# Opening of an attention and feed-forward kernel: order of the first tile's products, count of warm transposes, place of GpSimd's first subtractions, table of the loads' landing

## The chip, the cores and the metric

The kernel runs on one core of a Trainium2 chip. A core has five engines with queues of their own: TensorE (matrix products and transposes into PSUM), VectorE, ScalarE, GpSimd and SyncE (SP), which issues most transfers. The metric is the time of one execution in microseconds (us) of device time, the median over several runs. In the profile's rows TensorE is PE (its weight load is PEld), VectorE DVE, ScalarE ACT, GpSimd POOL.

## What is computed

The reference normalizes x and feeds it to two branches, a dilated local attention and a feed-forward network with SiLU:

```python
def _A_ref(x, wqkv, wo):                     # H = 32 heads of 20, W = 8 keys, dil = 2
    q, k, v = split(x @ wqkv)
    logits = jnp.einsum("bhsd,bhswd->bhsw", q, kg) * scale      # kg: keys at s, s-2, ..., s-14
    attn = _softmax(jnp.where(mask, logits, -1e9), axis=-1)
    o = jnp.einsum("bhsw,bhswd->bhsd", attn, vg)
    return merge(o) @ wo

def _B_ref(x, w1, w2):
    return jnp.einsum("bsf,fd->bsd", _silu(jnp.einsum("bsd,df->bsf", x, w1)), w2)

xn = _layernorm(x, axis=-1)
s = _A_ref(xn, A_wqkv, A_wo)
g = _silu(_B_ref(xn, B_w1, B_w2))
return x + s * g
```

x is 2048 x 640, wqkv 640 x 1920, w1 640 x 1536, everything float32.

## The kernel before

**Groups and tiles.** The 2048 tokens are worked in four groups of 512, each of four tiles (T = 4) of 128 tokens. In a group come four quarters of the q, k, v product (eight heads each, 480 columns), with the attention of each quarter on VectorE; then the feed-forward network, and the output product of the group before. TensorE's order is the order in which the program adds its work.

**Three products for one.** A float32 operand is split into a high part, rounded for TensorE, and a low part, the difference. Each product is done as high x high, low x high and high x low. For activations the parts are `th` and `tl`: ScalarE copies a transposed tile from PSUM into th (L674), VectorE subtracts (L678). For weights ScalarE copies the loaded tile into the high half of a ring tile `w` (L445), and VectorE or GpSimd subtracts into its low half (L451). The ring has seven tiles; in the built program they are called w_75 to w_81, and the first five chunks of the first quarter lie in w_75 to w_79. Chunks 0 and 1 are subtracted by GpSimd, chunks 2, 3, 4 by VectorE (`ON_DVE`).

**The opening** (`first_quarter`). TensorE first turns the identity 20 times (`WARM`, L644). Meanwhile x of the first tile lands in two halves, one issued by SP and one by ScalarE. `begin(t)` puts a tile's layer norm on VectorE: two statistics (L656), their aggregate (L657), a square root on ScalarE (L495), a reciprocal (L497), and the normalization itself (L661) in two parts, of three and two chunks of 128 columns. `turn(t)` transposes the five chunks on TensorE (L670) into two PSUM tiles, and queues the copies into th and tl. `products(t, steps)` adds products (L691); a step (k, c) is pass k (0: th with the high weight, 1: tl with the high weight, 2: th with the low weight) of chunk c. For tile 0 the order is th and tl of each chunk in turn; between tile 1's transposes and its first product stand `NOW` products of pass 2 of tile 0.

**The planner.** `Weave` collects every operation with its engine, a modelled duration, the keys that it reads and writes and a priority, and sorts each engine's queue by a modelled time line; `emit` then writes the instructions in that order. The keys serve the planner alone: the semaphores in the built program are set by the framework below it, from the memory that instructions really share. Each engine's queue is in order. A transfer's end is modelled from its bytes (`RATE`), a constant (`LAND`), and a correction for early ones (`EARLY`). Operations marked `lock` are modelled as excluding each other between VectorE and GpSimd.

**Transfers.** SP issues, in the opening, x of tile 0 (half), weight chunk 0, x of tile 1, chunks 2 to 4, x of tile 2, two chunks of the next quarter (`xr`, for w_80 and w_81), x of tile 3, four more (`gate`), then stores of split weights (`half_q`) and further loads. ScalarE issues the other half of x and weight chunk 1. There are eight lanes: a transfer waits on SP until the one eight places before it has landed.

Of the kernel before, what the change touches and what calls it, by code (L numbers as in the profile page):

```python
# [8 lines left out]
F32 = mybir.dt.float32  # L9
F32R = mybir.dt.float32r  # L10
AF = mybir.ActivationFunctionType
OP = mybir.AluOpType
# [10 lines left out]
T = 4  # L23
# [7 lines left out]
NS = 3  # L31
SINGLE = 6
RAW_AHEAD = 10
WARM, WARM2 = 20, 3
HOLD = 3.4
LO = 10
HALVES = 1
BY_ACT = (1,)
QAT = 48
MORE = 32  # L40
# [1 line left out]
X_AT = 3, 6, 8  # L42
TILE_AT = 1, 1.5, 5, 6
LOW_AT = 3
NOW = 1
ON_DVE = (2, 3, 4)


# [16 lines left out]
class Weave:  # L65
# [8 lines left out]
    LANES = 8  # L74
    RATE = 310e3
    LAND = 1.9
    EARLY = 10.0, -0.4
    TABLE = 1.28
    PATIENCE = 1.0

# [28 lines left out]
    def order(self):  # L109
        engines = ("PE", "POOL", "DVE", "ACT", "SP")  # L110
        free = dict.fromkeys(engines, 0.0)
        can = {e: [] for e in engines}
        tensor = [o for o in self.ops if o.eng == "PE"]
        at = 0
        lock = dma = 0.0
        lanes = {e: [0.0] * self.LANES for e in ("SP", "POOL", "ACT")}
        table = held = None
        for o in self.ops:
            if o.left == 0:
                can[o.eng].append(o)  # L120
        done = []
        while len(done) < len(self.ops):
            best = None
            for e in engines:
                if e == "PE":
                    c = [tensor[at]] if at < len(tensor) and tensor[at].left == 0 else []
                else:
                    c = can[e]
                if not c:
                    continue  # L130
                f = free[e]
                est = [max(f, o.ready, lock if o.lock else 0.0, lanes[e][0] if o.nbytes else 0.0) for o in c]
                m = min(est)
                if best is None or m < best[0] or (m == best[0] == lock and held == best[1].eng):
                    pick = min((o for o, t in zip(c, est) if t <= m + 1e-9), key=lambda o: (o.prio, o.seq))
                    if pick.prio >= 140:
                        soon = [(t, o.prio, o.seq, o) for o, t in zip(c, est)
                                if o.prio < 100 and t <= m + min(self.PATIENCE, pick.dur / 2)]
                        if soon:
                            m, _, _, pick = min(soon, key=lambda v: v[:3])  # L140
                            if best is not None and m >= best[0]:
                                continue
                    best = m, pick
            t, o = best
            e = o.eng
            o.start = t
            dur = o.dur
            if e == "ACT" and o.table is not None and o.table != table:
                table = o.table
                dur += self.TABLE  # L150
            free[e] = t + dur
            if o.nbytes:
                dma = max(dma, t + dur) + o.nbytes / self.RATE
                o.end = dma + self.LAND + (self.EARLY[1] if lanes[e][-1] and t < self.EARLY[0] else 0.0)
                lanes[e] = lanes[e][1:] + [o.end]
            else:
                o.end = t + dur
                if o.lock:
                    lock, held = o.end, e
            if e == "PE":  # L160
                at += 1
            else:
                can[e].remove(o)
            done.append(o)
            for u in o.users:
                u.left -= 1
                u.ready = max(u.ready, o.end + (self.HOP if u.eng != e or o.nbytes else 0.0))
                if u.left == 0:
                    can[u.eng].append(u)
        self.span = max(o.end for o in done)  # L170
        return sorted(done, key=lambda o: (o.start, o.seq))
# [7 lines left out]
def local_attention_silu_ffn(ctx: ExitStack, tc: tile.TileContext, x, wqkv, wo, w1, w2, out):  # L179
# [80 lines left out]
    def dve(n, fn, reads, writes, prio, lock=False):  # L260
        add("DVE", dv(n), fn, reads, writes, prio, lock)
# [4 lines left out]
    def pe(dur, fn, reads, writes):  # L266
        add("PE", dur, fn, reads, writes)
        clock[0] += dur
# [152 lines left out]
    def w_load():  # L421
        i = loaded[0]
        if i >= len(units):
            return
        loaded[0] += 1
        u, s = units[i], i % RING
        n = width(i)
        r = WR[s]
        at = start(i)
        both = r.rearrange("p (s d) -> p s d", s=2)[:, :, at:at + n]  # L430
        whi, wlo = both[:, 0], both[:, 1]
        kh, kl = ("wh", s), ("wl", s)
        due = clock[0]
        if what[i] == "load":
            src = halves[u]
            add("POOL", 1.0, lambda: nc.gpsimd.dma_start(both, src), [("half", u), ("half", u, "more")], [kh, kl], due + 10,  # L436
                nbytes=2 * n * P * 4)
            raws_due(i, sum(j < i for j in fresh) - 1)
            return
        k = fresh.index(i)  # L440
        if not k:
            raw_load(0)
            rawn[0] = 1
        raw, kr = raws.pop(i)
        act(n, lambda: nc.scalar.activation(whi, raw, AF.Copy), kr + [("sd", 0)] * (k < 2), [kh], 1000 + due)  # L445
        pool_does = k < LO and k not in ON_DVE
        eng, cost, by = ("POOL", po(n), nc.gpsimd) if pool_does else ("DVE", dv(n), nc.vector)
        parts = HALVES if pool_does and k < DC else 1
        for j in range(parts):
            cs = slice(j * n // parts, (j + 1) * n // parts)  # L450
            add(eng, po(n // parts) if pool_does else cost, lambda cs=cs: by.tensor_tensor(  # L451
                out=wlo[:, cs], in0=raw[:, cs], in1=whi[:, cs].bitcast(F32), op=OP.subtract), [kh] + kr,
                [kl if j == parts - 1 else kl + (j,)], due if pool_does else LOW_AT if k < LO else 50, lock=True)
        if what[i] == "store":
            def keep(to, a, b, key):
                dma(lambda: nc.sync.dma_start(to, both[:, :, a:b].bitcast(F32)), [kh, kl], [key], 2 * (b - a) * P * 4,
                    due + 25)
            wide = width(len(units) - 1 - units[::-1].index(u))
            kept = dram.tile([P, 2, wide], F32, name="half_" + "_".join(map(str, u)))
            halves[u] = kept  # L460
            past = n - wide if u[0] == "q" and u[1] == NQ - 1 else 0
            keep(kept[:, :, :n - past], past, n, ("half", u))
            for k in range(past // MORE):
                v = ("q", k, u[2])
                keep(halves[v][:, :, 3 * CQ:], k * MORE, (k + 1) * MORE, ("half", v, "more"))
        raws_due(i, k)
# [26 lines left out]
    def ln_rstd(a, b, at=1):  # L493
        n = range(a, b)
        act(b - a, lambda: nc.scalar.activation(SD[:, 0, a:b], MV[:, a:b, 1], AF.Sqrt, bias=epst, scale=1.0),  # L495
            [("mv", t) for t in n], [("sd", t) for t in n], 0, "sqrt")
        dve(10, lambda: nc.vector.reciprocal(out=SD[:, 1, a:b], in_=SD[:, 0, a:b]),  # L497
            [("sd", t) for t in n], [("rs", t) for t in n], at)
# [139 lines left out]
    def first_quarter(i):  # L638
# [3 lines left out]
        def warm(n, where):  # L642
            for k in range(n):
                nc.tensor.transpose(where[:, tsl(k % T)], ident, ident)  # L644
        pe(4.5, lambda: warm(WARM, ROT[0]), ["consts"], [("rot", 0)])

        PARTS = (0, 3), (3, DC)

        def begin(t):

            at = TILE_AT[t]
            st, ks = ST[t % 2], ("st", t % 2)
            for k in range(2):
                cs = slice(k * 320, (k + 1) * 320)
                kx = ("xin", t) if t or k else ("xin", t, "a")
                dve(320, lambda k=k, cs=cs: nc.vector.bn_stats(out=st[:, k, :], in_=XIN[:, t, cs]), [kx], [ks + (k,)], at)  # L656
            dve(60, lambda: nc.vector.bn_aggr(out=MV[:, t, :], in_=st), [ks + (0,), ks + (1,)], [("mv", t)], at)  # L657
            ln_rstd(t, t + 1, at)
            for j, (a, b) in enumerate(PARTS):
                cs = slice(a * P, b * P)  # L660
                dve((b - a) * 64, lambda cs=cs: nc.vector.tensor_scalar(  # L661
                    out=XIN[:, t, cs], in0=XIN[:, t, cs], scalar1=MV[:, t, 0:1], scalar2=SD[:, 1, t:t + 1],
                    op0=OP.subtract, op1=OP.mult), [("rs", t), ("mv", t), ("xin", t)], [("xn", t, j)], at, lock=True)
# [50 lines left out]
            ps[t] = b, kp  # L714
        turn(0)
        pe(0.11 * WARM2, lambda: warm(WARM2, ACC[5]), [], [("acc", 5)])
        products(0, [(k, c) for c in range(DC) for k in (0, 1)])
        turn(1)
        products(0, [(2, c) for c in range(NOW)])
        products(1, passes(0, 1))  # L720
# [292 lines left out]
```

## Time and profile before

| | |
|---|---|
| time, median of 3 runs | 637.09 us (636.86 to 637.24) |
| time of the profiled execution | 638.26 us |
| its span (first to last instruction) | 636.5 us |
| TensorE busy | 629.1 us, 99% of the span, 3495 products |
| VectorE busy | 545.8 us, 86%, 548 instructions |
| ScalarE busy | 224.0 us, 35% |
| GpSimd busy | 114.6 us, 18% |

A row of the time line gives the start, the duration (of all merged instructions), engine, line, operation, written tile <- read tiles, shape, and xN for N merged instructions; brackets give the idle time before it and what ended it. A row of waits reads "engine line waited for: us in total, times, longest us". A row of windows gives the stretch, its length, then the busy time and the number of instructions of PE, PEld, DVE, ACT and POOL, then the granted TensorE clock (1.00 is full), the share and the rate of the DMA engines. A row of one line's instructions gives durations in ns as least/median/greatest. Products are pipelined: one that lasts 0.38 us is followed by the next after about 0.22.

### The profile page before, as it was taken

How to read it: one execution, taken by the hardware profiler on the slowest of the kernel's cores; microseconds unless marked ns; L12 is line 12 of the kernel's file. 1: busy time of each engine (PE TensorE's matmuls, PEld its weight loads, DVE VectorE, ACT ScalarE, POOL GpSimd, SP SyncE). 2: the span in 40 equal slices, each digit the busy share in tenths (PEclk: the TensorE clock that was granted, in tenths of full speed). 3: DMA queues.
4: the chain of work that ended last, by engine and by line, in shares of the span. 5: the costliest groups of instructions: out<-in, count | busy, mean ns of one | idle time of the engine just before them, and what ended most of it. 6: DMA issues, size and time to landing. Idle time of an engine off the chain costs nothing.

```text
span 636.5 us, 9095 instructions
## 1 busy us (share of the span) xinstructions
PE 629.1 (99%) x3495; PEld 569.4 (89%) x3495; DVE 545.8 (86%) x548; ACT 224.0 (35%) x461; POOL 114.6 (18%) x159
## 2 busy tenths in 40 slices
PE   7999999999999999999999999999999999999997
PEld 6888899998889999999888999999988999999997
DVE  6699999999898979999969999999704999999734
ACT  4535555453436123232523512233313231223230
POOL 4410000011110162112221104311222211111100
PEclk8999999999999999999999999999999999999999
DMA  9899999868997988566798999766779999656652
GB/s 295 292 304 293 318 404 406 303 184 251 307 313 227 291 261 279 171 200 202 201 251 211 320 356 318 248 200 186 217 191 271 248 312 260 182 193 190 192 179 83
DMA packets 77500, 160.82 MB, mean 253 GB/s; under 512 B 9248, under 2 KB 38912, under 8 KB 77456
## 3 DMA queue, kind: packets, MB, share of 16 engines
q0 software_dynamic: 25952, 79.31, 42.9%
q1 hardware_dynamic: 50960, 80.52, 39.5%
q8 instruction: 27, 0.44, 0.3%
q10 hardware_dynamic: 544, 0.41, 0.2%
q14 instruction: 17, 0.14, 0.1%
HBM read 107.91 MB, written 34.16 MB: 223 GB/s over the span
## 4 chain that ended last, share of the span: by engine, by line
PE 98%; DVE 1%; DMA 1%; ACT 0%; issue 0%
PE acc L781 22%; PE acc L783 15%; PE acc L750 10%; PE acc L749 10%; PE acc L748 10%; PE rot L905 9%; PE rot L907 9%; PE rot L906 9%; PE rot L511 2%; PE acc L691 2%; DMA xin<-in_A_x_dram 1%; DVE st L656 0%; DVE xin L661 0%; PE rot L670 0%; PE rot L891 0%; PE rot L631 0%
## 5 line engine op out<-in xcount | busy, mean ns | idle before, releaser
L573 DVE TENSOR_TENSOR pr<-q,kv 128x2560 f32<-128x2560 f32 x32 | 90.2, 2820 | 32.5 <-DMA kv<-kv 32.3
L748 PE MATMUL acc<-w,th 128*128 128x512 f32 (+2 forms) x300 | 113.4, 378 | 0.0
L781 PE MATMUL acc<-w,sh 128*128 128x384 f32 x384 | 113.2, 334 | 0.0
L750 PE MATMUL acc<-w,th 128*128 128x512 f32 (+2 forms) x300 | 113.0, 377 | 0.0
L749 PE MATMUL acc<-w,tl 128*128 128x512 f32 (+2 forms) x300 | 112.9, 376 | 0.0
L783 PE MATMUL acc<-w,sh 128*128 128x256 f32 x384 | 107.2, 279 | 0.0
L905 PE MATMUL rot<-th,w 128*128 128x512 f32 x240 | 95.9, 400 | 0.0
L907 PE MATMUL rot<-th,w 128*128 128x512 f32 x240 | 93.9, 391 | 0.0
L906 PE MATMUL rot<-tl,w 128*128 128x512 f32 x240 | 93.7, 390 | 0.0
L605 DVE TENSOR_TENSOR pr<-e,kv 128x2560 f32<-128x2560 f32 x32 | 90.3, 2823 | 0.7
L576 DVE TENSOR_REDUCE l<-pr 128x128 f32<-128x2560 f32 x32 | 90.1, 2816 | 0.4
L436 POOL DMA_DIRECT2D w<-half_q x52 | 37.4, 719 | 237.6 <-DMA xr<-in_A_wqkv_dram 93.3
L436 POOL DMA_DIRECT2D w<-half_w x72 | 38.5, 534 | 212.0 <-PE acc L783 89.2
L610 DVE TENSOR_TENSOR pr<-pr 128x1280 f32<-128x1280 f32 x64 | 73.8, 1153 | 1.0
L783 PEld LDWEIGHTS acc<-w,sh 128*128 128x128 f32 x384 | 72.2, 188 | 1.0
L781 PEld LDWEIGHTS acc<-w,sh 128*128 128x128 f32 x384 | 72.1, 188 | 1.0
L918 ACT ACTIVATE sh<-rot 128x512 fp32r<-128x512 f32 x48 | 28.7, 598 | 125.4 <-PE rot L907 125.4
L750 PEld LDWEIGHTS acc<-w,th 128*128 128x128 f32 x300 | 56.3, 188 | 8.7
L749 PEld LDWEIGHTS acc<-w,tl 128*128 128x128 f32 x300 | 56.3, 188 | 8.6
L748 PEld LDWEIGHTS acc<-w,th 128*128 128x128 f32 x300 | 56.4, 188 | 8.5
L781 PE MATMUL acc<-w,sl 128*128 128x384 f32 x192 | 57.8, 333 | 0.0
L532 ACT ACTIVATE kv<-acc 128x320 f32<-128x320 f32 x64 | 28.3, 442 | 74.2 <-PE acc L750 71.6
(96 smaller groups left out, 1021.3 us busy)
## 6 DMA issues: line engine op xcount, KB each, us to landing
w<-half_w POOLq DMA_DIRECT2D x72, 640.0 KB, 5.0
w<-half_q POOLq DMA_DIRECT2D x39, 512.0 KB, 4.9
half_w<-w SPq DMA_DIRECT2D x24, 640.0 KB
kv<-kv SPq DMA_DIRECT2D x16, 560.0 KB
kv<-kv SPq DMA_DIRECT2D x16, 420.0 KB
w<-half_wo POOLq DMA_DIRECT2D x10, 640.0 KB, 5.1
gate<-in_B_w_dram SPq DMA_DIRECT2D x16, 320.0 KB
w<-half_q POOLq DMA_DIRECT2D x13, 384.0 KB, 5.2
```

The source lines that it names most:

```text
L436: add("POOL", 1.0, lambda: nc.gpsimd.dma_start(both, src), [("half", u), ("half", u, "more")], [kh, kl], due + 10, nbytes=2 * n * P * 4)
L573: dve(2560, lambda t=t: nc.vector.tensor_tensor(out=PR, in0=win(qq[:, t:t + 2, :], W, 0), in1=win(kv[:, 0, t:t + 2, :], W, CQ), op=OP.mult ...
L576: dve(2560, lambda t=t: nc.vector.tensor_reduce(out=l[:, t:t + 2].rearrange("p t w h -> p (t w h)"), in_=PR.rearrange("p t w (h d) -> p (t ...
L605: dve(2560, lambda t=t, v=v: nc.vector.tensor_tensor(out=PR.rearrange("p t w (h d) -> p t (w h) d", d=DH), in0=e[:, t:t + 2].rearrange("p ...
L748: nc.tensor.matmul(o, hi, wh, start=c == 0, stop=False)
L749: nc.tensor.matmul(o, lo, wh, start=False, stop=False)
L750: nc.tensor.matmul(o, hi, wl, start=False, stop=c == DC - 1)
L781: nc.tensor.matmul(a[t][0][:, :CA], st, w[:, :CA], start=first, stop=last)
L783: nc.tensor.matmul(b[t // 2][0][:, h * CB:(h + 1) * CB], st, w[:, CA:], start=first and h == 0, stop=last, skip_group_check=True)
L905: nc.tensor.matmul(h, wh[:, cs], TH[i][:, c, :], start=c == 0, stop=False)
L906: nc.tensor.matmul(h, wh[:, cs], TL[i][:, c, :], start=False, stop=False)
L907: nc.tensor.matmul(h, wl[:, cs], TH[i][:, c, :], start=False, stop=c == DC - 1)
```

## The change

- `WARM` goes from 20 to 28, and its modelled duration from 4.5 to 5.1.
- Tile 0's ten products follow a list, `FIRST`: th of chunks 0 and 1, tl of chunks 0 and 1, and then th and tl of chunks 2, 3 and 4 in turn.
- `NOW` goes from 1 to 3: three products of pass 2 of tile 0 stand between tile 1's transposes and its first product.
- GpSimd's subtractions of chunks 0 and 1 read the key `("xn", 0, 1)`, the second part of tile 0's normalization. `HALVES`, which was 1, goes.
- The ends of the first nine transfers are a table in `EARLY`.
- The aggregate, square root and reciprocal of a tile have priority -1, and the statistics of the last tile read the reciprocal of the one before.

```diff
-WARM, WARM2 = 20, 3
+WARM, WARM2 = 28, 3
-HALVES = 1
+FIRST = (0, 0), (0, 1), (1, 0), (1, 1), (0, 2), (1, 2), (0, 3), (1, 3), (0, 4), (1, 4)
-NOW = 1
+NOW = 3
-    EARLY = 10.0, -0.4
+    EARLY = 3.9, 3.8, 4.9, 5.3, 6.05, 6.95, 7.7, 8.4, 9.4
...
-                o.end = dma + self.LAND + (self.EARLY[1] if lanes[e][-1] and t < self.EARLY[0] else 0.0)
+                o.end = self.EARLY[moved] if moved < len(self.EARLY) else dma + self.LAND
+                moved += 1
...
-        parts = HALVES if pool_does and k < DC else 1
-        for j in range(parts):
-            cs = slice(j * n // parts, (j + 1) * n // parts)
-            add(eng, po(n // parts) if pool_does else cost, lambda cs=cs: by.tensor_tensor(
-                out=wlo[:, cs], in0=raw[:, cs], in1=whi[:, cs].bitcast(F32), op=OP.subtract), [kh] + kr,
-                [kl if j == parts - 1 else kl + (j,)], due if pool_does else LOW_AT if k < LO else 50, lock=True)
+        wait = [("xn", 0, 1)] if pool_does and k < DC else []
+        add(eng, cost, lambda: by.tensor_tensor(out=wlo, in0=raw, in1=whi.bitcast(F32), op=OP.subtract),
+            [kh] + kr + wait, [kl], due if pool_does else LOW_AT if k < LO else 50, lock=True)
...
-        pe(4.5, lambda: warm(WARM, ROT[0]), ["consts"], [("rot", 0)])
+        pe(5.1, lambda: warm(WARM, ROT[0]), ["consts"], [("rot", 0)])
...
-                dve(320, lambda ...: nc.vector.bn_stats(...), [kx], [ks + (k,)], at)
-            dve(60, lambda: nc.vector.bn_aggr(out=MV[:, t, :], in_=st), [ks + (0,), ks + (1,)], [("mv", t)], at)
-            ln_rstd(t, t + 1, at)
+                turn_of = [("rs", t - 1)] if t == T - 1 else []
+                dve(320, lambda ...: nc.vector.bn_stats(...), [kx] + turn_of, [ks + (k,)], at)
+            dve(60, lambda: nc.vector.bn_aggr(out=MV[:, t, :], in_=st), [ks + (0,), ks + (1,)], [("mv", t)], -1)
+            ln_rstd(t, t + 1, -1)
...
-        products(0, [(k, c) for c in range(DC) for k in (0, 1)])
+        products(0, FIRST)
```

What the built program's queues look like after it, in the opening: TensorE differs as the lists say. ScalarE copies w_75 before w_76 (the other way round before), takes tile 1's square root ahead of w_77, and copies w_80 ahead of tile 1's th. VectorE takes tile 1's aggregate ahead of tile 0's tl, all three weight subtractions behind tile 1's normalization, one half of tile 2's statistics ahead of tile 1's tl, and tile 3's statistics behind tile 2's normalization. GpSimd subtracts w_75 before w_76, and its first subtraction waits for the same two things as before, its load and ScalarE's copy. SP puts the load of `xr` ahead of the second weight store, and the next group's x behind two more weight loads. Behind the opening, VectorE's, ScalarE's and SP's queues hold the same work in an order that differs in places, and ScalarE has two table loads fewer.

More of the change, by code (lines that the diff above doesn't have):

```diff
@@ L113, in order @@
         tensor = [o for o in self.ops if o.eng == "PE"]
-        at = 0
+        at = moved = 0
         lock = dma = 0.0
@@ L655, in begin @@
                 kx = ("xin", t) if t or k else ("xin", t, "a")
-                dve(320, lambda k=k, cs=cs: nc.vector.bn_stats(out=st[:, k, :], in_=XIN[:, t, cs]), [kx], [ks + (k,)], at)
-            dve(60, lambda: nc.vector.bn_aggr(out=MV[:, t, :], in_=st), [ks + (0,), ks + (1,)], [("mv", t)], at)
-            ln_rstd(t, t + 1, at)
+                turn_of = [("rs", t - 1)] if t == T - 1 else []
+                dve(320, lambda k=k, cs=cs: nc.vector.bn_stats(out=st[:, k, :], in_=XIN[:, t, cs]), [kx] + turn_of, [ks + (k,)], at)
+            dve(60, lambda: nc.vector.bn_aggr(out=MV[:, t, :], in_=st), [ks + (0,), ks + (1,)], [("mv", t)], -1)
+            ln_rstd(t, t + 1, -1)
             for j, (a, b) in enumerate(PARTS):
```

## The prediction

> **What bounds the kernel now.** I read the chain of waits first, then the waits of TensorE, then the first 26 us in order of time, then the granted clock.
>
> ```profile
> span 636.5 us, 9095 instructions
> PE 98%; DVE 1%; DMA 1%; ACT 0%; issue 0%
> ...
> PE rot L670 <- DVE xin L661: 2.0, 3, 1.1
> ...
> PEld acc L691 <- ACT th L674: 0.4, 1, 0.4
> ```
>
> TensorE is the chain, and after the first tiles it waits for nobody: all its waits lie in the first quarter (three on the normalization L661, one on the th copy). Whatever this change gives or takes is the moment at which the first quarter ends; the first product of the second quarter starts at 25.09.
>
> ```profile
> 1.37 3.72 PE L644 MATMUL rot<-ident 128*128 128x128 f32 x20 [1.37 <-POOL ident masks.py:199]
> ...
> 6.21 0.55 PE L670 MATMUL rot<-ident,xin 128*128 128x128 f32 x3 [1.12 <-DVE xin L661]
> 7.43 0.63 PE L670 MATMUL rot<-ident,xin 128*128 128x128 f32 x2 [0.67 <-DVE xin L661]
> 10.10 0.60 PE L691 MATMUL acc<-w,th 128*128 128x480 f32 x1
> 10.50 0.59 PE L691 MATMUL acc<-w,tl 128*128 128x480 f32 x1
> 11.81 0.71 PE L670 MATMUL rot<-ident,xin 128*128 128x128 f32 x5
> 12.27 1.96 PE L691 MATMUL acc<-w,th 128*128 128x480 f32 x6
> 14.07 1.24 PE L691 MATMUL acc<-w,tl 128*128 128x480 f32 x5
> 16.36 0.77 PE L670 MATMUL rot<-ident,xin 128*128 128x128 f32 x5 [0.18 <-DVE xin L661]
> 20.20 0.71 PE L670 MATMUL rot<-ident,xin 128*128 128x128 f32 x5
> 25.09 0.38 PE L748 MATMUL acc<-w,th 128*128 128x480 f32 x1
> ```
>
> To be seen: the warm transposes end at 5.09, the first tile's transposes come in two parts at 6.21 and 7.43, products then start every 0.40 us, and from 14.07 five of them start 0.215 apart (1.24 less one length of 0.38, over four). That factor of two is the clock:
>
> ```profile
> 0.71:4.12 3.41, 2.75 (x13) 2.75 (x14) 0.54 (x10) 1.49 (x2) 2.40 (x3) 1.00 0.60 175
> 4.12:7.54 3.42, 1.64 (x13) 1.16 (x12) 2.99 (x7) 1.84 (x4) 1.52 (x2) 1.00 1.05 326
> 7.54:10.95 3.41, 3.41 (x12) 3.00 (x13) 3.36 (x10) 2.04 (x5) 0.90 (x1) 0.50 1.08 351
> 10.95:14.36 3.41, 3.27 (x18) 2.62 (x17) 2.37 (x6) 1.75 (x4) 0.69 (x1) 1.00 1.13 341
> ```
>
> The stretches are 3.41 us long. The third ran at 0.50. The second, the one judged before it, had TensorE busy 1.64 of 3.42 us (48%); the first had 2.75 (81%), and behind it the pace doubled (13 of the 20 transposes in 2.75 us, the other 7 in 0.97).
>
> **The change part by part.**
>
> ```profile
> 5.68 1.70 DVE L661 TENSOR_SCALAR xin<-xin,mv,sd 128x384 f32<-128x384 f32 x2
> 7.29 0.87 DVE L656 BATCH_NORM_STATS2 st<-xin 128x6 f32<-128x320 f32 x2
> 9.88 0.80 DVE L661 TENSOR_SCALAR xin<-xin,mv,sd 128x384 f32<-128x384 f32 x2
> 10.60 1.22 DVE L451 TENSOR_TENSOR w<-pr,w 128x480 fp32r<-128x480 f32 x2
> 12.86 0.89 DVE L678 TENSOR_TENSOR tl<-rot,th 128x384 fp32r<-128x384 f32 x2 [1.04 <-ACT th L674]
> 13.67 0.88 DVE L656 BATCH_NORM_STATS2 st<-xin 128x6 f32<-128x320 f32 x2
> 14.70 0.83 DVE L656 BATCH_NORM_STATS2 st<-xin 128x6 f32<-128x320 f32 x2
> L661 DVE TENSOR_SCALAR xin<-xin,mv,sd x8: 401/475/1299, 5.7 to 18.7; 128x384 f32<-128x384 f32 x4, 128x256 f32<-128x256 f32 x4
> ...
> 6.02 2.41 POOL L451 TENSOR_TENSOR w<-pr,w 128x480 fp32r<-128x480 f32 x2 [2.80 <-ACT w L445]
> ...
> 5.35 1.15 ACT L445 ACTIVATE w<-pr 128x480 fp32r<-128x480 f32 x2
> 5.89 0.60 ACT L445 ACTIVATE w<-pr 128x480 fp32r<-128x480 f32 x1
> 6.80 0.49 ACT L674 ACTIVATE th<-rot 128x384 fp32r<-128x384 f32 x1 [0.30 <-PE rot L670]
> 9.36 0.28 ACT L495 ACTIVATE sd<-mv,epst 128x1 f32<-128x1 f32 x1
> 9.54 0.59 ACT L445 ACTIVATE w<-pr 128x480 fp32r<-128x480 f32 x1
> 12.99 1.10 ACT L445 ACTIVATE w<-xr 128x480 fp32r<-128x480 f32 x2
> ...
> 9.52 0.87 SPq L410 DMA_DIRECT2D gate<-in_A_wqkv_dram  x1
> 11.18 0.56 SPq L456 DMA_DIRECT2D half_q<-w  x1
> 12.55 0.39 SPq L482 DMA_DIRECT2D xin<-in_A_x_dram  x1
> ```
>
> 1. *GpSimd behind the normalization.* The second part of the first tile's normalization began at 7.38 - 1.30 = 6.08 and took 1.299 us where others take 0.40: GpSimd's two subtractions (from 6.02, 1.2 us each) had the port. The new key orders only the planner's list; in the built program GpSimd's instruction still waits for its load and ScalarE's copy alone. So the edit does not do what it says. But the plan also swaps ScalarE's two copies: w_75 now comes first, and before its copy began at 5.89, 0.54 behind the other (two others: 1.10 in all, 0.6 long, so 0.50 apart), which reads as a copy that waited for its load. Then GpSimd starts at 5.89 + 0.67 = 6.56 (the lag from 5.35 to 6.02), the normalization is through at 6.48, and the transposes of part two come at about 6.5 instead of 7.43. Queued behind the waiting copy on ScalarE are w_76 and the first th copy, which moves from 6.80 to about 6.9; the first product waits for it, at 7.45 or so, and part 3 hides that. If that load lands by 5.35 the collision stays as it was, and this part gives nothing. I take the later, since the row shows 5.89.
>
> 2. *28 warm transposes.* Eight more, at 0.09 (five in 12.27 - 11.81) to 0.14 us (7 in 0.97), end at 5.8 to 6.2: not past 6.21. They raise the second stretch to at least 1.64 + 0.74 = 2.4 us (70%), and part two at 6.5 adds about 0.6: some 85%. That is past the 81% that raised the clock, so I take it that the third stretch runs at full clock. Bounds: nothing, or products at 0.215 instead of 0.40 for some seven, 1.3 us; a loss would need them past 6.21.
>
> [...]
>
> 3. *FIRST.* The ten products keep their number; th of chunks 0 and 1 come ahead of their tl. VectorE now puts the aggregate of tile 1 ahead of the first tl (0.2 us), ScalarE its square root (0.28) ahead of w_77. At full clock: stats as before, if x of tile 1 landed no earlier than used, to 8.16; tl at 8.3 to 8.8; third product 8.8. ScalarE: w_77 at 8.6, w_78 9.1, w_79 at 9.66 (its load is there by 9.52, where SP's next issue on that lane stands), done 10.25. Products in pairs behind each copy: 9.2, 9.75, 10.3, 10.5; the tile-1 transposes at 10.73 instead of 11.81. Gained: 1.08. The normalization of tile 1 ends near 10.05 and covers it.
>
> 4. *NOW = 3, w_80 ahead, statistics of tile 3 behind the reciprocal of tile 2.* Three low products run at 11.19, 11.41 and 11.63, in place of one and a wait of 0.44; VectorE's w_77 (one of three, 0.61 apart, from 10.05) is there. But ScalarE now copies w_80 ahead of tile 1's th, and sits on its load: SP's store at 11.18 needs the same lane, so it has landed by then; I take 11.1. The th copy is then done at 11.1 + 0.50 + 0.49 = 12.1, first th product 12.14, a wait of 0.3. In before that product stands at 12.27 + 0.22 + 0.44 = 12.93. Twelve products at 0.22 (two of the low ones are already done) lead to 14.78. VectorE: from the end of tl (13.75) to tile 2's transposes (16.36) it took 2.61, of which 0.83 was tile 3's statistics and half of 0.88 now stands ahead: 1.34, so from 13.0 to 14.35; GpSimd's w_80 and w_81 (11.9 and 13.1, 1.2 each) hold the port to 14.3, which costs up to 0.4. So 14.8 against 16.36: 1.56.
>
> 5. *Behind that.* From 16.36 to 25.09 TensorE has 8.73 us of work. Its next need is tile 3's normalization, at 14.8 + 3.84 = 18.6; VectorE gets there by about 17.9 (0.8 statistics, two tl, 0.8 normalization from 15.1). Cover 0.7. SP moves the next group's x load behind two weight loads, from 12.55 to about 15: it feeds statistics that stand behind the whole opening on VectorE, and if it is late it delays VectorE alone. Table and priorities cost nothing themselves; they re-sort VectorE, ScalarE and SP through the first 300 us, and no TensorE wait stands there to be gained.
>
> Sum: 636.5 - 1.56 = 634.9 span; the profiled execution's 638.26 becomes 636.7. The median shown is 637.09, 1.17 below that execution; I carry the difference over: 635.5, rounded to 635.6 for the hand-over times between engines that I left out.
>
> **The rivals.**
>
> *The clock falls at 7.54 all the same.* Then products run at 0.40 to 10.95, part 3 gives 0 to 0.3, part 4 0.8 (th of tile 1 needs no wait: transposes 11.81, copy done 12.83, first th 12.93, twelve products, 15.57). 636.2. For it: how much is enough is known only as between 48 and 81%. Against: 85%.
> [...]
>
> *It falls one stretch later.* With waits before 8.8 and 10.3 the stretch to 10.95 is perhaps 70 to 85% busy. Half clock to 14.36 makes eight products of 0.40 after the transposes; the rest ends at about 16.0: gain 0.4, 636.7.
>
> *The timed runs never had the fall.* The profiled execution is 1.17 longer than the median, about what the fall costs. Then only the wait of 0.44 is to be had, less the new 0.3 and plus VectorE's shorter way: 0.3, 636.8.
>
> *Slower: VectorE's re-sorted list.* In several places a long attention product now stands ahead of a subtraction. The tightest:
>
> ```profile
> 62.93 2.82 DVE L573 TENSOR_TENSOR pr<-q,kv 128x2560 f32<-128x2560 f32 x1
> 65.67 0.82 DVE L451 TENSOR_TENSOR w<-gate,w 128x640 fp32r<-128x640 f32 x1
> ...
> 71.25 0.39 PE L907 MATMUL rot<-th,w 128*128 128x512 f32 x1
> ```
>
> Another product of 2.82 us (2.74 to the next start) comes ahead of this subtraction (w_76, an early feed-forward weight). It would end at 66.49 + 2.74 = 69.2 if VectorE is not earlier, and TensorE, 1.55 earlier, wants it at 69.7: 0.5 left. Any further lateness x costs x - 0.5; from 2.1 us the kernel is slower than before. At 2.8 it is 637.8. Against it: VectorE's waits before that point are for ScalarE behind TensorE, so it moves up too.
>
> **How the numbers follow.** Forecast 0.57 (635.6; its own range 635.2 to 636.0, from the landing of w_80's load and the port), clock falls at 7.54 0.07, later 0.11, timed runs without it 0.10, slower 0.15. Faster or slower means 0.2%, about what can be told from no change: 1.27 us, so below 635.82. Of the forecast 0.5 lies below it: faster 0.50; same 0.07 + 0.07 + 0.11 + 0.10 = 0.35; slower 0.15. The range leaves out most of slower and the forecast's low tail: 635.1 to 637.1.
>
> **What would show it.** Right: second part of the first transposes near 6.5; normalization x8 with no 1.3 us entry before 9; granted clock 1.00 from 7.54 to 10.95; tile-1 transposes near 10.7 and tile-2 near 14.8; the first product of the second quarter near 23.5; no TensorE wait behind it. Wrong: a 0.50 stretch anywhere after 7.5; GpSimd's first subtraction before 6.1; a TensorE wait on w or th past 20 us.

## The result, and the profile after

The changed kernel takes 636.56 us (median of 22 runs, 636.11 to 637.41) against 637.23 us for the kernel before on the same chip (22 runs): a ratio of 0.9985, 95% interval 0.9978 to 0.9992. That is 0.15% faster (0.67 us or 0.11% between the medians), less than the 0.2% that was set as the bound of what can be told from no change, and 1.0 us above the forecast of 635.6. The profiled executions moved as summed: 638.26 to 636.80, and their spans 636.5 to 635.0 (634.9 was predicted). So the sum held for the execution that it was made against, and the error lies between that execution and the median. The mean of the same runs falls more than the median, from 637.51 to 636.55.

Chain, waits of TensorE, then TensorE's first 24 us, of the kernel after:

```profile
span 635.0 us, 9113 instructions
PE 99%; DVE 0%; POOL 0%; issue 0%; POOLq 0%
PE rot L642 <- POOL ident masks.py:199: 1.4, 1, 1.4
```

```profile
1.38 6.15 PE L642 MATMUL rot<-ident 128*128 128x128 f32 x28 [1.38 <-POOL ident masks.py:199]
7.37 0.71 PE L669 MATMUL rot<-ident,xin 128*128 128x128 f32 x5
8.44 0.71 PE L690 MATMUL acc<-w,th 128*128 128x480 f32 x2
9.04 0.70 PE L690 MATMUL acc<-w,tl 128*128 128x480 f32 x2
...
10.98 0.71 PE L669 MATMUL rot<-ident,xin 128*128 128x128 f32 x5
11.44 2.21 PE L690 MATMUL acc<-w,th 128*128 128x480 f32 x8
...
15.01 0.71 PE L669 MATMUL rot<-ident,xin 128*128 128x128 f32 x5
...
23.68 0.38 PE L747 MATMUL acc<-w,th 128*128 128x480 f32 x1
```

The tile-1 transposes come at 10.98 instead of 11.81, tile 2's at 15.01 instead of 16.36, and the second quarter at 23.68 instead of 25.09, 1.41 us sooner; the spans differ by 1.5. From there to the end both kernels take 611.3 to 611.4 us. The three waits for the normalization (2.0 us) are gone from the list of TensorE's waits.

The same stretches of 3.41 us as before the change, in the view of windows (busy time of PE, PEld, DVE, ACT and POOL, then the granted clock):

```profile
0.71:4.12 3.41, 2.74 (x13) 2.74 (x14) 0.72 (x10) 1.49 (x2) 2.40 (x3) 1.00 0.67 182
4.12:7.54 3.42, 3.42 (x19) 3.42 (x18) 1.86 (x7) 1.39 (x3) 0.84 (x1) 1.00 1.04 318
7.54:10.95 3.41, 3.37 (x18) 2.29 (x17) 3.38 (x10) 2.49 (x6) 1.55 (x2) 1.00 1.09 363
```

No half clock behind 7.5. But the 28 warm transposes took 6.15 us, 0.22 each: to the end at the slow pace that the trace before shows ahead of its rise (13 in 2.75 us, then 7 in 0.97). The first record of full clock in this trace stands at 7.32 us; in the trace before it stood at 4.12. (The column says 1.00 where the trace has no record yet, so the pace tells.) The rise does not come at the same place of the program in each execution, it is 3.20 us apart in these two, and this is the thing that the prediction lacked.

VectorE, ScalarE and GpSimd in the opening of the kernel after:

```profile
5.50 0.80 DVE L660 TENSOR_SCALAR xin<-xin,mv,sd 128x384 f32<-128x384 f32 x2
7.43 0.89 DVE L655 BATCH_NORM_STATS2 st<-xin 128x6 f32<-128x320 f32 x2 [1.13 <-DMA xin<-in_A_x_dram]
8.48 0.50 DVE L677 TENSOR_TENSOR tl<-rot,th 128x384 fp32r<-128x384 f32 x1
...
14.38 0.80 DVE L660 TENSOR_SCALAR xin<-xin,mv,sd 128x384 f32<-128x384 f32 x2
...
11.27 0.61 ACT L446 ACTIVATE w<-xr 128x480 fp32r<-128x480 f32 x1 [0.89 <-DMA xr<-in_A_wqkv_dram]
11.78 0.75 ACT L673 ACTIVATE th<-rot 128x384 fp32r<-128x384 f32 x2
...
6.70 2.39 POOL L450 TENSOR_TENSOR w<-pr,w 128x480 fp32r<-128x480 f32 x2 [3.47 <-ACT w L446]
```

GpSimd begins at 6.70, behind the normalization, which now takes 0.80 us and is through at 6.30: the collision is gone, as forecast. In this trace its gain is not to be seen on TensorE. The first tl, which the third product waits for, stands behind tile 1's statistics, and these wait for x of tile 1 until 7.43.

### The profile page after: what moved, and what is told of

The parts are those of the page before. It is cut to its first block, busy times and chain, and to the rows that moved or that the text cites. A ratio compares the mean times of both kernels' runs of the same rounds, so it can differ in the third digit from the quotient of the medians.

```text
span 635.0 us, 9113 instructions
## 1 busy us (share of the span) xinstructions
PE 629.7 (99%) x3503; PEld 570.1 (90%) x3503; DVE 538.1 (85%) x548; ACT 220.6 (35%) x459; POOL 112.9 (18%) x159
## 4 chain that ended last, share of the span: by engine, by line
PE 99%; DVE 0%; POOL 0%; issue 0%; POOLq 0%
PE acc L780 22%; PE acc L782 15%; PE acc L748 10%; PE acc L749 10%; PE acc L747 10%; PE rot L904 9%; PE rot L906 9%; PE rot L905 9%; PE rot L509 2%; PE acc L690 2%; PE rot L642 1%; PE rot L669 0%; PE rot L890 0%; PE rot L629 0%; DVE gate L858 0%; DVE xin L860 0%
## 5 line engine op out<-in xcount | busy, mean ns | idle before, releaser
L906 PEld LDWEIGHTS rot<-th,w 128*128 128x128 f32 x240 | 45.0, 188 | 9.9
```

Source lines behind the costliest of these rows:

```text
L906: nc.tensor.matmul(h, wl[:, cs], TH[i][:, c, :], start=False, stop=c == DC - 1)
```

## The experiments

**The kernel before once more.** Nothing is edited; only the profile is taken again.

> The kernel before, unchanged, profiled once more. Theory A (two kinds of execution): three times in four it is one of the lower kind, about 637.1, with no stretch at half clock behind the first rise, TensorE's first product of the second quarter near 23.9 to 24.1 instead of 25.09, and 611.3 us from there to the end as in every trace so far. If it is again one of the upper kind, 638.2 or more, it shows the fall again. Theory C (the kinds come from elsewhere): a time near 637.1 with the fall still in it and the first product of the second quarter at 25.1.

It took 637.21 us, span 635.4. TensorE, then the windows by this execution's own stretches:

```profile
1.38 4.07 PE L644 MATMUL rot<-ident 128*128 128x128 f32 x20 [1.38 <-POOL ident masks.py:199]
...
7.47 0.44 PE L670 MATMUL rot<-ident,xin 128*128 128x128 f32 x2 [0.67 <-DVE xin L661]
...
10.78 0.71 PE L670 MATMUL rot<-ident,xin 128*128 128x128 f32 x5
...
15.34 0.77 PE L670 MATMUL rot<-ident,xin 128*128 128x128 f32 x5 [0.19 <-DVE xin L661]
...
24.07 0.38 PE L748 MATMUL acc<-w,th 128*128 128x480 f32 x1
```

```profile
1.42:4.84 3.42, 3.42 (x16) 3.42 (x17) 0.84 (x4) 1.49 (x2) 1.80 (x1) 1.00 0.84 233
4.84:8.25 3.41, 1.94 (x14) 1.36 (x13) 2.98 (x8) 2.19 (x6) 2.19 (x2) 1.00 1.07 345
```

Products stand 0.22 apart from 9.04 on and the second quarter starts at 24.07, a full 1.02 us sooner than in the execution that the prediction was worked out from. This is the third rival's case. The kernel before has two kinds of execution: of its 110 runs in all comparisons, 80 lie between 636.86 and 637.78 (median 637.17) and 30 between 638.0 and 638.93 (median 638.3). The profiled 638.26 was of the upper kind. The granted clock of 88 of these runs is on record. Of the 23 upper ones among them 17 show 0.997, and one stretch of 3.41 us at half clock makes just that (0.5 x 3.41 / 636.5 = 0.0027 lost); no lower one shows less than 0.999. The other six, at 638.0 to 638.29, show 0.999 and so no such stretch behind the first record. A rise that came late would look like this, since the time before the first record does not count (the execution of the trace after, slow to 7.32, shows 1.000), but none of the six was traced. Here the first rise came at 4.84, and the 3.41 us behind it were 57% busy (1.94 of 3.41): full clock stayed on behind them, where half clock came behind 48%.

**28 warm transposes alone.**

```diff
 (kernel before)
-WARM, WARM2 = 20, 3
+WARM, WARM2 = 28, 3
```

> The kernel before with 28 warm transposes for 20 and nothing else (the planned length of 4.5 left, so every other engine's list is as before). Theory A, the third rival's: the times of the kernel before are of two kinds (636.9 to 637.4 and 638.1 to 638.7) because the 3.41-us stretches do not begin at the same place of the program in each execution, and only where a boundary falls near 7.5 us does the clock fall; the warm transposes are what removes that. Then the upper kind is gone, all times lie between 636.4 and 637.4, and the median is at or a little under the lower kind, 636.8 to 637.2. Theory B, the prediction's way of carrying over: the profiled execution simply stands 1.2 us above the timed ones, and the clock falls in all of them; then all times drop by the 1.1 us of the clock, to a median of 636.0. Theory C: the two kinds have nothing to do with the opening; then a third of the times stays above 638 and the median stays at 637.2.

637.12 us (636.68 to 637.52, 11 runs), ratio 0.9995 (0.9986 to 1.0004): the upper kind is absent and the median stays at the lower kind. Theory A's numbers; the 1.1 us of the clock (theory B) are not in the median.

**The change with 20 warm transposes.**

```diff
 (kernel after)
-WARM, WARM2 = 28, 3
+WARM, WARM2 = 20, 3
...
-        pe(5.1, lambda: warm(WARM, ROT[0]), ...
+        pe(4.5, lambda: warm(WARM, ROT[0]), ...
```

> The changed kernel with 20 warm transposes for 28 (all other engines' lists as changed). Theory A: two kinds of times again, the lower at 636.2 to 636.7 and an upper one some 1.2 us above it (637.4 to 638.0), in about a third of the executions; median 636.5 to 636.7. Theory B: the clock falls always, all times near 637.5. Theory C: nothing changes, one kind, 636.5.

636.6 us (636.05 to 638.22). One run of 11 lies at 638.22 (its granted clock is 1.000, so the record shows no fall in it), three more at 637.05 to 637.42, seven at 636.7 or less. So the median is the same with 20 as with 28, and the upper kind is rarer than the third expected; 11 runs do not tell one in eleven from one in four.

**12 warm transposes.**

```diff
 (kernel before)
-WARM, WARM2 = 20, 3
+WARM, WARM2 = 12, 3
```

> The kernel before with 12 warm transposes for 20, nothing else. Theory A: the fewer warm transposes, the more often a stretch of 3.41 us in the opening is empty enough for the clock to stay low or fall: the upper kind (638.1 to 638.8, a quarter of the executions with 20) comes in half of them or more, and the median is 637.6 to 638.8. Theory C: the share of the upper kind stays at a quarter, median 637.2.

638.19 us (637.69 to 639.79, 12 runs), ratio 1.0014 (1.0005 to 1.0022); no run is left at 637.2. Its profiled execution shows the low clock staying on, TensorE first, then windows:

```profile
1.38 2.82 PE L644 MATMUL rot<-ident 128*128 128x128 f32 x12 [1.38 <-POOL ident masks.py:199]
8.90 0.60 PE L691 MATMUL acc<-w,tl 128*128 128x480 f32 x1
9.30 0.60 PE L691 MATMUL acc<-w,th 128*128 128x480 f32 x1
...
12.50 0.71 PE L670 MATMUL rot<-ident,xin 128*128 128x128 f32 x5
```

```profile
2.26:5.67 3.41, 1.94 (x10) 1.54 (x8) 1.31 (x5) 1.66 (x4) 0.96 (x1) 1.00 0.96 300
5.67:9.08 3.41, 2.60 (x10) 2.13 (x11) 3.41 (x8) 2.29 (x6) 2.42 (x2) 1.00 1.06 347
9.08:12.50 3.42, 3.42 (x10) 2.69 (x9) 2.69 (x7) 1.06 (x3) 0.00 (x0) 1.00 1.11 350
```

Products are 0.40 apart until 12.5, where the first record of full clock stands. Behind a stretch 76% busy (2.60 of 3.41) the clock stayed low; behind the next one, busy throughout (3.42 of 3.42), it was full. Half of the 12 runs lie at 638.3 or above, as theory A expected. The other half lie at 637.69 to 638.07, where the kernel before has next to none; theory A did not have that, and no trace shows one of them. What holds is that long executions become rarer from 12 to 20 to 28 warm transposes (six of 12 at 638.3 or above, 30 of 110 at 638.0 or above, none of 11 above 637.52), as it says.

**NOW = 1.**

```diff
 (kernel after)
-NOW = 3
+NOW = 1
```

> The changed kernel with NOW = 1: one low product of tile 0 ahead of tile 1's th products instead of three, two of them behind. By the prediction's fourth part TensorE then waits for the th copy longer by the two products that stood ahead, 0.37 + 0.43 = 0.80 us in the trace after instead of 0.37, and all that follows is 0.43 later, less what the wait of 0.2 for tile 2's normalization hides: median +0.2 to +0.43, 636.8 to 637.0. Rival: what is gained there is taken back by the next wait (tile 2's normalization ends when it does): no difference, 636.5 to 636.6.

637.06 us (636.65 to 637.55), ratio 0.9994 (0.9985 to 1.0003): 0.50 us above the changed kernel. Nearly the whole gain of the median goes.

**The old order of the first ten products.**

```diff
 (kernel after)
-        products(0, FIRST)
+        products(0, [(k, c) for c in range(DC) for k in (0, 1)])
```

> The changed kernel with the old order of tile 0's first ten products (th and tl of each chunk in turn). By the prediction's third part, FIRST itself counted little beside the clock: th, then a wait for tl to about 9.04, then nine products 0.215 apart end where they ended, near 10.98, so 0 to 0.1 later: median 636.5 to 636.7. Rival: the order of the products is what gained the opening's time, the tile-1 transposes come 0.4 us or more later and the median is 636.9 to 637.2.

636.46 us (636.19 to 636.94), ratio 0.9986 (0.9978 to 0.9995): FIRST by itself is worth nothing that these runs can tell (0.10 below the changed kernel).

**TensorE's order alone.**

```diff
 (kernel before)
-WARM, WARM2 = 20, 3
+WARM, WARM2 = 28, 3
-NOW = 1
+NOW = 3
-        products(0, [(k, c) for c in range(DC) for k in (0, 1)])
+        products(0, FIRST)
```

> The kernel before with TensorE's order alone as changed (FIRST and NOW = 3) and 28 warm transposes, so that the clock does not fall; planner, table, keys and priorities are as before, and VectorE still has tile 3's statistics ahead of tile 2's normalization. The prediction's fourth part needs both: the low products fill the wait for tile 1's th copy, and the statistics moved away let tile 2's normalization come earlier. Then here the next wait, for that normalization (L662), takes back what the low products gain: tile-2 transposes as in the kernel before with 28 warm transposes (4.56 us behind the tile-1 transposes, 3.98 of it work), median 637.0 to 637.1. Rival: the order of the products is enough by itself: 4.0 to 4.2 us between the two, median 636.5 to 636.7.

637.11 us (636.84 to 637.31), ratio 0.9996 (0.9987 to 1.0005): nothing gained over 637.12 with 28 warm transposes alone. TensorE and VectorE of this run:

```profile
10.75 0.71 PE L671 MATMUL rot<-ident,xin 128*128 128x128 f32 x5
...
15.30 0.77 PE L671 MATMUL rot<-ident,xin 128*128 128x128 f32 x5 [0.59 <-DVE xin L662]
...
13.65 0.83 DVE L657 BATCH_NORM_STATS2 st<-xin 128x6 f32<-128x320 f32 x2
14.58 0.99 DVE L662 TENSOR_SCALAR xin<-xin,mv,sd 128x384 f32<-128x384 f32 x2
```

The wait for tile 1's th is gone, and in its place TensorE waits 0.59 for tile 2's normalization, which stands behind tile 3's statistics (13.65). In the changed kernel these come behind it: there tile 2's transposes follow tile 1's by 4.03 us, here by 4.55. NOW = 3 and the changed lists of the other engines are one gain: with either alone the kernel stays at 637.1 (here, and with NOW = 1). That within these lists it is the place of tile 3's statistics rests on the rows; no run moved them alone.

**One more low product ahead.**

```diff
 (kernel after)
-NOW = 3
+NOW = 4
```

> The changed kernel with NOW = 4: one more low product of tile 0 ahead of tile 1's th products; every other engine's list is as in the changed kernel. The wait for tile 1's th copy (0.37 in the trace after, 0.44 longer with NOW = 1) should shrink by one product of 0.215. If nothing else holds, the first product of the second quarter comes 0.2 earlier (23.05 to 23.1 where the traces with 20 and 28 warm transposes had 23.27 to 23.31) and the median is 636.3 to 636.4. Rival: tile 2's normalization, whose first part is ready near 14.45 to 14.6, stops the transposes there: gain 0 to 0.1, median 636.5 to 636.6.

636.52 us (636.3 to 636.8), ratio 0.9982 (0.9974 to 0.9991): 0.04 below the changed kernel, the rival's case. Tile 2's normalization starts at 14.38 in its trace, as in the changed kernel's, and the tile-2 transposes come at 14.91 instead of 15.01.

**Tile 1's th copies ahead of w_80.**

```diff
 (kernel after)
-    EARLY = 3.9, 3.8, 4.9, 5.3, 6.05, 6.95, 7.7, 8.4, 9.4
+    EARLY = 3.9, 3.8, 4.9, 5.3, 6.05, 6.95, 7.7, 8.4, 9.4, 10.4, 11.1, 11.8, 12.7
```

> The changed kernel with four more entries in the planner's table of landings (10.4, 11.1, 11.8, 12.7, as the trace has them): ScalarE's list then has tile 1's two th copies ahead of the copy of w_80, which stands and waits for its load to 10.9 in the trace after. If that copy is what the first th product of tile 1 waits for (0.37 in the trace after), the wait goes and all that follows comes 0.3 to 0.4 earlier: first product of the second quarter at 22.9 to 23.3, median 636.1 to 636.3. Rival: the next wait, for tile 2's normalization on VectorE, takes it back: 636.5 to 636.6.

636.99 us (636.72 to 638.62), ratio 0.9997 (0.9989 to 1.0006): a miss. It shows two things, on TensorE and ScalarE:

```profile
15.00 0.77 PE L669 MATMUL rot<-ident,xin 128*128 128x128 f32 x5 [0.58 <-DVE xin L660]
...
23.72 0.38 PE L747 MATMUL acc<-w,th 128*128 128x480 f32 x1
69.84 0.50 PE L904 MATMUL rot<-th,w 128*128 128x512 f32 x1 [0.25 <-ACT sf L918]
...
66.65 0.74 ACT L446 ACTIVATE w<-xr 128x640 fp32r<-128x640 f32 x1 [2.55 <-DMA half_q<-w]
```

The wait for th is gone, but VectorE now does tl of tile 1 ahead of tile 2's statistics, and TensorE waits 0.58 for that normalization: taken back. And further on the longer table re-sorted ScalarE, which sits 2.55 us on a buffer with a weight copy ahead of the copies that TensorE needs; from there this run is 0.57 us later than the trace after, where it was level at 69.4. Two of its 11 runs are 1.3 to 1.6 us above its median; of the 110 runs with 28 warm transposes no others are more than 1 us above theirs. Their granted clock is 1.000, so the record shows no fall in them, and their cause is open.

**Without the key on GpSimd's subtractions.**

```diff
 (kernel after)
-        wait = [("xn", 0, 1)] if pool_does and k < DC else []
+        wait = []
```

> The changed kernel without the key that puts GpSimd's first subtractions behind the normalization. The orders of the opening are the same with it and without it on every engine; some 240 lines of VectorE's list and 57 of ScalarE's change places further on. By the prediction's first part the key orders the planner's list alone and does nothing: 636.4 to 636.7, and GpSimd's first subtraction still begins behind the normalization, at 6.6 to 6.9. Rival: the lists further on matter (the slower rival's mechanism), then a wait of TensorE past 20 us and 637 or more.

637.81 us (637.66 to 637.98), ratio 1.0006 (0.9997 to 1.0014), 1.25 above the changed kernel. The opening is as good as any (second quarter at 23.31). The loss comes at 145 us; TensorE, then VectorE:

```profile
145.03 0.45 PE L780 MATMUL acc<-w,sl 128*128 128x384 f32 x1 [0.85 <-DVE sl L919]
...
141.56 2.82 DVE L574 TENSOR_REDUCE l<-pr 128x128 f32<-128x2560 f32 x1
144.29 0.68 DVE L919 TENSOR_TENSOR sl<-sf,sh 128x512 fp32r<-128x512 f32 x1
```

And VectorE of the changed kernel at the same place:

```profile
142.20 0.69 DVE L919 TENSOR_TENSOR sl<-sf,sh 128x512 fp32r<-128x512 f32 x1
142.81 2.81 DVE L574 TENSOR_REDUCE l<-pr 128x128 f32<-128x2560 f32 x1
```

A long reduction stands ahead of the subtraction sl that TensorE waits for; with the key it stands behind. It is the slower rival's mechanism, 75 us behind the place that was named for it.

**Without the new table.**

```diff
 (kernel after)
-    EARLY = 3.9, 3.8, 4.9, 5.3, 6.05, 6.95, 7.7, 8.4, 9.4
+    EARLY = 10.0, -0.4
...
-                o.end = self.EARLY[moved] if moved < len(self.EARLY) else dma + self.LAND
+                o.end = dma + self.LAND + (self.EARLY[1] if lanes[e][-1] and t < self.EARLY[0] else 0.0)
```

> The changed kernel with the old table of two numbers in the planner. ScalarE copies w_76 ahead of w_75 again. By the prediction's first part GpSimd's subtractions then begin near 6.0 and the second part of the first normalization takes 1.2 to 1.3 us again, so the second part of the first transposes comes at 7.3 to 7.5 instead of 6.2 to 6.5. If the first tl (behind the statistics that wait for tile 1's x) is what the products wait for, as the traces of the changed kernel have it, this costs nothing at the second quarter: 23.2 to 23.7, 636.4 to 636.7, unless the lists further on bring a wait of TensorE past 20 us (as without the key: 1.2 us). Rival: the earlier normalization is worth what it gained on VectorE: second quarter 0.5 us or more later.

638.38 us (638.15 to 638.67), ratio 1.0011 (1.0002 to 1.0019), 1.82 above the changed kernel. VectorE and TensorE of its opening, and its later wait:

```profile
5.81 1.70 DVE L660 TENSOR_SCALAR xin<-xin,mv,sd 128x384 f32<-128x384 f32 x2
7.43 0.87 DVE L655 BATCH_NORM_STATS2 st<-xin 128x6 f32<-128x320 f32 x2
...
7.57 0.44 PE L669 MATMUL rot<-ident,xin 128*128 128x128 f32 x2 [0.67 <-DVE xin L660]
...
10.96 0.71 PE L669 MATMUL rot<-ident,xin 128*128 128x128 f32 x5
...
23.71 0.38 PE L747 MATMUL acc<-w,th 128*128 128x480 f32 x1
...
145.86 0.44 PE L780 MATMUL acc<-w,sl 128*128 128x384 f32 x1 [1.29 <-DVE sl L919]
```

The collision is back (1.70 us for the two normalizations, second transposes at 7.57), and yet the tile-1 transposes stand at 10.96 and the second quarter at 23.71, 0.03 from the trace after. These two traces do not settle what the earlier normalization is worth, though. Tile 1's statistics start at 7.43 in both: here directly behind the normalization, with no wait for x, in the trace after because x landed only then. The seven traces with the early normalization give an estimate. With the collision the statistics could start 1.62 us behind the start of the normalization (7.43 - 5.81 here). Without it they started when x landed, which was 0.22 sooner than that with the longer table (5.53 + 1.62 - 6.93), 0.10 with the old order, 0.03 with 20 warm transposes, and later than that in the other four. So the earlier normalization earns from nothing to about 0.2 us, by when x lands, and in the trace after it earned nothing. Against that trace this run loses 1.6 us, all of it at the same sl at 145 us, waited for 1.29 us. Of the 1.82 between the medians this leaves 0.2, which may lie in the opening; no trace shows it.

## Why the prediction was right and wrong

*The sum and the median.* The step that failed is "I carry the difference over". The 1.17 us between the profiled execution and the median was no constant. It was the clock: its fall stands in the profile and in 17 of the 23 upper runs whose clock is on record, and in no lower one. Against the lower kind (637.17) the change gives 0.6 us, against the upper (638.3) 1.7. The third rival had this, with 0.3 for the gain and a chance of 0.10; its own row, "about what the fall costs", spoke for it and deserved more. 636.56 lies in the range because the range reached to that rival; that is luck, not a merit of the sum. There is luck in the profiled executions' 636.80 for 636.7 too. The steps behind it came later than summed (first transposes at 7.37 for 6.5, third product at 9.04 for 8.8), since the clock rose late and x of tile 1 landed late in that execution; with x earlier, the second quarter was reached at 23.27 to 23.31, where the sum gives 25.09 - 1.56 = 23.53.

*Part 1.* Right in its steps (GpSimd at 6.70 for 6.56, normalization through at 6.30 for 6.48). No trace shows a port; what stands in them is the length: 1.70 us for the two normalizations in the six traces with GpSimd's subtractions from 5.96 to 6.16 on, 0.80 to 0.81 in the seven with them from 6.69 to 6.92 on; for tile 2's two, 0.99 where they begin beside them (15.63 in the trace before) and 0.80 behind them (14.38 in the trace after), which is 0.19 for the 0.4 that part 4 allowed. But it is worth little, since part 3 took x of tile 1 to land no later than it was used before. In the changed kernel's lists the third product comes 1.61 us behind the start of tile 1's statistics, and these start when x lands: 7.43 and 9.04 in the trace after; with NOW = 1

```profile
7.47 0.89 DVE L655 BATCH_NORM_STATS2 st<-xin 128x6 f32<-128x320 f32 x2 [1.03 <-DMA xin<-in_A_x_dram]
...
9.08 0.70 PE L690 MATMUL acc<-w,tl 128*128 128x480 f32 x2 [0.79 <-DVE tl L677]
```

and with 20 warm transposes

```profile
7.07 0.89 DVE L655 BATCH_NORM_STATS2 st<-xin 128x6 f32<-128x320 f32 x2 [0.79 <-DMA xin<-in_A_x_dram]
...
8.68 0.70 PE L690 MATMUL acc<-w,tl 128*128 128x480 f32 x2 [0.23 <-DVE tl L677]
```

So the products move by 0.4 with the landing of x from one execution to the next, and the earlier normalization earns 0.2 at most in these traces (see the run without the table). "The edit does not do what it says" holds for the opening: its orders are the same with and without the key. That the key does nothing at all is wrong: further on it decides 1.25 us.

*Part 2.* The clock behind 7.54 was right, also why: more warm transposes take the emptiest stretch away (behind the first rise TensorE is busy 77 to 99% of 3.41 us in the nine traces with 28, 48 and 57% in the two of the kernel before), and the upper kind with it (none of the 11 runs with 28 alone). Its size, 1.3 us at most, belongs to about a quarter of the executions (30 of 110, by their times). "Not past 6.21" was wrong: where full clock comes late (7.32 in the trace after), 28 last to 7.53 and push the first transposes to 7.37. That cost nothing in that trace, the tl being later still. The two rivals with a clock that falls at 7.54 or 10.95 did not come about in any trace with 28.
In the trace before the fall came behind a stretch 48% busy whose longest gap was 1.12 us (5.09 to 6.21). In the trace after warm transposes, and nothing else, filled the stretch from 3.91 to 7.32 (3.41 of 3.41 us busy), and full clock came behind it.

*Part 3.* Its 1.08 us was the clock's, not the order's: the changed kernel with the old order takes 636.46, and the kernel before, in the execution whose clock did not fall, has its tile-1 transposes at 10.78 without any change (10.73 was forecast, 11.81 is the trace before).

*Part 4.* Right, and most of the gain of the median. The terms beyond part 3 were 1.56 - 1.08 = 0.48; NOW = 1 takes 0.50 back. w_80 ahead of th costs the 0.3 forecast. The wait stands at TensorE's weight load in the trace after:

```profile
12.30 0.95 PEld L690 LDWEIGHTS acc<-w,th 128*128 128x128 f32 x5 [0.37 <-ACT th L673]
```

The eight products around it take 2.21 us, where seven distances of 0.215 and a length of 0.38 make 1.88: 0.33 lost. It isn't worth mending, because tile 2's normalization is next.

*Part 5.* Right: 611.3 us from the second quarter to the end, in the changed kernel and in every run with its lists. But "table and priorities cost nothing themselves" holds for these lists alone: the old table costs 1.6 us behind the opening, the longer one 0.5, no key 1.25. The slower rival named the right mechanism and the wrong place: three of the five re-sorted programs here (no key, no table, longer table) lost time to it or its like on ScalarE, the changed kernel and the one with NOW = 1 did not, and no trace shows TensorE waiting for the w_76 subtraction.

No run beats the changed kernel beyond the noise (636.46 with the old order, 636.52 with NOW = 4). What is left to gain in the opening is small: from 7.37 to 23.68 are 16.31 us, of which 60 products of 0.215 and 23 transposes of 0.093 (five in 11.44 - 10.98) make 15.0; and the waits that were taken away in these runs (NOW = 4, the longer table) gave way to the next one.

## What to carry to other kernels

Before carrying a profiled execution's sum over to the median, look whether the two are of the same kind; a profile that stands 0.2% above the median (638.26 against 637.09 here) may hold a stall that most runs don't have, and taking it away then moves the longer runs and not the median. In a chain of hand-overs, name for each gain the wait that ends just behind it: two edits that each earn nothing can be one gain together. Where a planner sorts the whole program from modelled times, an edit in its opening re-sorts everything behind, so the waits far from the edit are part of its price.

## What the runs showed of the hardware

In the trace before the records of the clock stand 3.41 us apart: full at 4.12, half at 7.54, full again at 10.95. In the other traces the shares here are of stretches of that length, laid back and on from the first record of full clock. That the share of one stretch decides the clock of the next is the author's reading; what the traces show is which clock came behind which share. The place of the first record differs from one execution to the next: it stands at 4.12 and 4.84 us in the two traces of the kernel before, and between 4.12 and 7.32 (the trace after) in the twelve traces with 20 or 28 warm transposes. By TensorE's busy share, full clock came behind 81% (the trace before) and the slow pace went on behind 74 to 76% (2.53 of 3.41 in the trace after's stretch from 0.50 to 3.91; 2.60 with 12 warm transposes); at full clock, it stayed behind 57% (the kernel before once more) and fell behind 48% (the trace before). So in these traces 76% did not end the slow pace, while 57% kept full clock. Landing times also differ between runs: the statistics that wait for x of tile 1 began at 6.89 in the run with the old order and at 7.47 with NOW = 1. The changed kernel's opening moves with them: its second quarter starts at 23.68 with x at 7.43, and at 23.27 with x at 7.07 (20 warm transposes).
